# Attention followed by a squared-ReLU MLP: the second product moved into row tiles between the scores, two head pairs at a time

## The chip, the core and the metric

The kernel runs on one core of a Trainium2 chip. The metric is the device time of one execution in microseconds; the median of three runs is given. The profiled execution is a run of its own, so its span is a little shorter than the device time.

A core has a matrix engine (PE, with its weight loads PEld), a vector engine (DVE), an activation engine (ACT), GpSimd (POOL) and 16 DMA engines fed from queues. Matmuls write to PSUM, which has eight banks of 512 float32 columns on 128 partitions.

Two words are used throughout. A matmul in a *column tile* has at most 64 output partitions and uses half of the array's columns; two of them, to partitions 0 to 63 and 64 to 127, run side by side. A matmul in a *row tile* has a contraction of 64 and uses half of the array's rows; two of them, with their operands on partitions 0 to 63 and 64 to 127, run side by side. A *full* matmul uses the whole array. In the profile's groups the two numbers with a star are contraction and output partitions: `128*128` is full, `128*64` and `112*64` are column tiles, `64*112` is a row tile.

## The reference

Eight batches, twelve heads (six pairs), 448 tokens, head size 64; then an MLP of 768 to 2048 to 768 over all 3584 tokens.

```python
def _attn_ref(q, k, v):                       # (8, 12, 448, 64) each
    scale = 1.0 / np.sqrt(q.shape[-1])
    scores = scale * np.matmul(q, k.transpose(0, 1, 3, 2))
    m = np.max(scores, axis=-1, keepdims=True)
    e = np.exp(scores - m)
    attn = e / (np.sum(e, axis=-1, keepdims=True) + np.exp(-m) + 1e-09)
    return np.matmul(attn, v)

def _moe_ref(x, w_in, w_out):                 # (3584, 768), (768, 2048), (2048, 768)
    h = x @ w_in
    r = np.maximum(h, 0.0)
    return (r * r) @ w_out
```

The output is float32; the kernel works in float16 with float32 sums in PSUM. The denominator is the sum of exponentials plus one (in a scaled form), so no maximum is taken.

## The kernel before

One *unit* is one head pair of one batch (batch 0 is cut into two halves of its query tokens, so it gives twelve smaller units; batches 1 to 7 give 42 full units). A unit has four blocks of keys, `kk` 0 to 3, two of them in each call of `scores`.

```python
def exp(out_, in_):
    nc.scalar.activation(out=out_, in_=in_, func=AF.Exp, scale=scale)

def scores(u, et, c):                         # cut to the case of batches 2 to 7
    for kk in (2 * c, 2 * c + 1):
        sp = s_psum.tile([P, 2, 512], FP32, name="sp")       # two such tiles, two banks each
        for h in range(2):
            for odd in range(2):
                r = slice(64 * odd, 64 * odd + 64)
                ...
                nc.tensor.matmul(sp[:, odd, h * (S // 2):(h + 1) * (S // 2)],
                                 qk[r, which, kx:kx + 2 * P - 1:2], qk[r, 0, x:x + S // 2],
                                 start=True, stop=True)      # row tiles, 224 columns
        exp(...)                                             # one 112x896 activation

def values(u, et, xp, o=0):                                  # column tiles, 448 columns
    for kk in range(RUN):
        for h in range(2):
            nc.tensor.matmul(xp[64 * h:64 * h + 64, o:o + n], vns[b][:, 2 * pr + h, kk, :], ...)

def row_sums(us, sums):                                      # column tiles against ones
    zp = m_psum.tile([128, 512], FP32, name="mp")
    ...
    nc.scalar.activation(out=rcp[:, 0:m], in_=zp[:, 0:m], func=AF.Ln, bias=one_b)
    nc.scalar.activation(out=rcp[:, 0:m], in_=rcp[:, 0:m], func=AF.Exp, scale=-1.0)

def product(out_, lhsT, rhs, start, stop):
    if halved[0]:                                            # two column tiles
        for x in (0, 64):
            nc.tensor.matmul(out_[x:x + 64], lhsT[:, x:x + 64], rhs, start=start, stop=stop)
    else:                                                    # full
        nc.tensor.matmul(out_, lhsT, rhs, start=start, stop=stop)
```

The MLP is cut into generators: `mlp_in` is the first product (six matmuls for each tile of 128 hidden rows, then ReLU and square on DVE), `mlp_out` the second (sixteen matmuls for each tile of 128 tokens by 512 or 256 output columns, then one scaled copy on ACT and a store). `drain(ns)` takes so many nanoseconds of such matmuls between the parts of a unit:

```python
for i in range(2 * NPAIR, NU + 1):
    ...
    scores(u, et, 0)
    if i in transpose_at:
        transposes(*transpose_at[i])
    drain(share[0] * 0.45)                    # full matmuls
    scores(u, et, 1)
    ...
    rcp = row_sums(done, (ess.pop(i - 1),))
    values(prev, ets.pop(i - 1), xp)
    halved[0] = u is not None
    drain(share[0] * 0.15)                    # column tiles from here
    for step in range(3):
        add_chunks(u, et, es, half, step)     # sums of exponentials over kk, on DVE
        drain(share[0] * (0.15, 0.1, 0.15)[step])
    halved[0] = False
    normalise(done, xp, rcp)
    take_up(i - 1)
drain(1e12)                                   # what is left of the MLP after the last unit
```

PSUM: two `sp` tiles of two banks, one bank for `xp`, three for everything called `mp`. Queries and keys of batches 0 and 1 are transposed on PE; those of the other batches are staged in DRAM in float16 and read back by transposing DMAs.

Of the kernel before, what the change touches and what calls it, by code (L numbers as in the profile page):

```python
# [11 lines left out]
ALU = mybir.AluOpType  # L12
# [3 lines left out]
def kernel(  # L16
# [19 lines left out]
    ON_PE = (0, 1)  # L36
    COLS = H * S // 2 + 16

# [11 lines left out]
    e_pool = ctx.enter_context(tc.tile_pool(name="e", bufs=2))  # L50
    es_pool = ctx.enter_context(tc.tile_pool(name="es", bufs=3))
    z_pool = ctx.enter_context(tc.tile_pool(name="z", bufs=1))
    g_pool = ctx.enter_context(tc.tile_pool(name="g", bufs=2))
# [10 lines left out]
    wout = persist.tile([128, NFFB, DM], FP16, name="wout")  # L64

# [15 lines left out]
    def load_natural(b, p0, p1):  # L81

        raw = b == 0 and p1 <= 3
        for n, r in (("q", q_r), ("k", k_r)):
            src = r[b, :, 2 * p0:2 * p1]
            if raw:
                t = nat.tile([P, 2, RUN, D], FP32, name=f"{n}r{p0}")
                (nc.sync if n == "q" else nc.scalar).dma_start(out=t, in_=src)
            else:
                if p0 % 3 == 0:  # L90
                    whole[n] = nat.tile([P, NPAIR, RUN, D], FP16, name=f"{n}n{p0 // 3}")
                t = whole[n][:, 2 * (p0 % 3):2 * (p0 % 3 + p1 - p0)]
                nc.gpsimd.dma_start(out=t, in_=src)
            for pr in range(p0, p1):
                naturals[n, b, pr] = t[:, 2 * (pr - p0):2 * (pr - p0) + 2]
# [5 lines left out]
    def load_wout(i, n):  # L101
        w = NFFB // n
        nc.gpsimd.dma_start(out=wout[:, i * w:(i + 1) * w, :], in_=wout_r[:, i * w:(i + 1) * w, :])
# [40 lines left out]
    def transposes(b, pr):  # L144
        tp = m_psum.tile([128, 2, 512], FP16, name="mp")
# [82 lines left out]
    def row_sums(us, sums):  # L228
# [3 lines left out]
        zp = m_psum.tile([128, 512], FP32, name="mp")  # L232
        for j, (u, es) in enumerate(zip(us, sums)):
            total = es[:, 0:2 * n]
            if n < S:
                total = total.rearrange("p (h n) -> p h n", h=2)
            for h in range(2):
                nc.tensor.matmul(zp[64 * h:64 * h + 64, j * n:(j + 1) * n], ones, of_head(total, u, h),  # L238
                                 start=True, stop=True)
# [5 lines left out]
    def normalise(us, xp, rcp):  # L245
        b, pr, q0, n = us[0]
        if b // 2 not in xts:
            xts[b // 2] = xt_pool.tile([128, DCH, 2 * S], FP16, name="xt")
        c = b % 2 * S + q0
        if len(us) == 1:  # L250
            nc.vector.tensor_mul(xts[b // 2][:, pr, c:c + n], xp[:, 0:n], rcp[:, 0:n])  # L251
        else:
            two = [t[:, 0:2 * n].rearrange("p (j n) -> p j n", j=2) for t in (xp, rcp)]
            nc.vector.tensor_mul(xts[b // 2][:, pr:pr + 2, c:c + n], *two)  # L254


    gts = {}
    halved = [False]

    def product(out_, lhsT, rhs, start, stop):  # L260

        if halved[0]:
# [5 lines left out]
    def mlp_in(t0, n):  # L268
        gt = gts[t0] = []
        xt, x0 = xts[t0 // (2 * S)], t0 % (2 * S)  # L270
        per = max(1, 512 // n) if n < 384 else 1
        for f0 in range(0, NFFB, per):
            hp = m_psum.tile([128, 512], FP32, name="mp")
            for j in range(per):
                fb = f0 + j
                for dc in range(DCH):
                    product(hp[:, j * n:(j + 1) * n], win[:, dc, fb * 128:(fb + 1) * 128],
                            xt[:, dc, x0:x0 + n], start=(dc == 0), stop=(dc == DCH - 1))
                    if j < per - 1 or dc < DCH - 1:
                        yield n / 2.4  # L280
            m = per * n
            rt = r_pool.tile([128, 512], FP16, name="rt")
            if t0 == 0 and f0 == 8:
                nc.scalar.activation(out=rt[:, 0:m], in_=hp[:, 0:m], func=AF.Relu)
            else:
                nc.vector.tensor_scalar(out=rt[:, 0:m], in0=hp[:, 0:m], scalar1=0.0, scalar2=None, op0=ALU.max)  # L286
            g = g_pool.tile([128, 512], FP16, name=f"g{f0}")
            nc.vector.tensor_mul(g[:, 0:m], rt[:, 0:m], rt[:, 0:m])  # L288
            for j in range(per):
                gt.append(g[:, j * n:(j + 1) * n])  # L290
            yield n / 2.4

    def store(c, ot, n0, n1):
        end = c + 128
        while c < end:
# [3 lines left out]
            t, p = c % S // (S // step), c % (S // step)  # L299
# [5 lines left out]
    def mlp_out(t0, n):  # L305
        gt = gts.pop(t0)
        for ts in range(n // 128):
            ot = osb_pool.tile([128, DM], FP32, name="ot")
            for n0, n1 in ((0, 512), (512, DM)):
                op = m_psum.tile([128, 512], FP32, name="mp")  # L310
                for fb in range(NFFB):
                    product(op[:, 0:n1 - n0], gt[fb][:, ts * 128:(ts + 1) * 128], wout[:, fb, n0:n1],
                            start=(fb == 0), stop=(fb == NFFB - 1))
                    if fb < NFFB - 1:
                        yield (n1 - n0) / 2.4
                nc.scalar.activation(out=ot[:, n0:n1], in_=op[:, 0:n1 - n0], func=AF.Copy, scale=OUT_SCALE)  # L316
                if n1 == DM or t0 + ts * 128 + 128 == NT:
                    store(t0 + ts * 128, ot, 0 if n1 < DM or t0 + ts * 128 + 128 < NT else n0, n1)
                if n1 < DM:
                    yield (n1 - n0) / 2.4  # L320
            yield (DM - 512) / 2.4
# [23 lines left out]
    load_v(1, 0, 3)  # L345
    for i in range(4):
        load_wout(i, 4)
    load_v(1, 3, 6)


    work, left = [], [0.0]

    def queue(part, t0, n):
        work.append((mlp_in if part == 1 else mlp_out)(t0, n))
        left[0] += (NFFB * DCH * n if part == 1 else n // 128 * NFFB * DM) / 2.4

    def drain(ns):
        while work and ns > 0:
            got = next(work[0], None)
            if got is None:  # L360
                work.pop(0)
            else:
                ns -= got
                left[0] -= got
# [6 lines left out]
    ready = {NPAIR - 1: [(1, 0, 128)],  # L371
             2 * NPAIR - 1: [(1, 128, 256), (2, 0, 128), (2, 128, 256)]}
    t0 = 384
    for b in range(1, B):
        n = 384 if b % 2 == 0 else 512
        ready[(b + 2) * NPAIR - 1] = [(1, t0, n), (2, t0, n)]
        t0 += n

    transpose_at = {pr - 1: (0, pr) for pr in range(1, NPAIR)}
    for pr in range(NPAIR):  # L380
        transpose_at[NPAIR + 2 + pr] = (1, pr)
# [6 lines left out]
    def take_up(i):  # L388
        if i in ready:
            for part in ready[i]:  # L390
                queue(*part)
            share[0] = left[0] / NPAIR

    share = [0.0]
    ets, ess = {}, {}
    xp = None
# [8 lines left out]
    for i in range(2 * NPAIR):  # L405
        u = units[i]
        et = ets[i] = e_pool.tile([P, RUN * 2 * S], FP16, name="et")
        es = ess[i] = es_pool.tile([P, 2 * S], FP16, name="es")
        half = e_pool.tile([P, 1024], FP16, name="half")
# [3 lines left out]
        halved[0] = True  # L413
# [3 lines left out]
        if i == NPAIR:  # L417
            values(units[i - 1], ets.pop(i - 1), xp, units[i - 1][3])
            rcp = row_sums(two, (ess.pop(i - 2), ess.pop(i - 1)))
            normalise(two, xp, rcp)  # L420
            take_up(i - 1)
            share[0] = left[0] / (NPAIR + 1)
# [9 lines left out]
        if two and i != NPAIR:  # L432
            rcp = row_sums(two, (ess.pop(i - 2), ess.pop(i - 1)))
        if i and i != NPAIR:
            values(units[i - 1], ets.pop(i - 1), xp, (i - 1) % 2 * units[i - 1][3])
        drain(share[0] * 0.3)
# [4 lines left out]
        drain(share[0] * 0.25)  # L441
        halved[0] = False


    for i in range(2 * NPAIR, NU + 1):
        u = units[i] if i < NU else None
# [4 lines left out]
        if u:  # L451
            b, pr = u[0:2]
            if pr == 0 and b + 1 < B:
                load_v(b + 1, 0, NPAIR)
                stage(b + 1)
            et = ets[i] = e_pool.tile([P, RUN * 2 * S], FP16, name="et")
            es = ess[i] = es_pool.tile([P, 2 * S], FP16, name="es")
            half = e_pool.tile([P, 1024], FP16, name="half")
            scores(u, et, 0)
            if i in transpose_at:  # L460
                transposes(*transpose_at[i])
            drain(share[0] * 0.45)
            scores(u, et, 1)
        if first:
            done = units[i - 2:i]
            values(prev, ets.pop(i - 1), xp, prev[3])
            rcp = row_sums(done, (ess.pop(i - 2), ess.pop(i - 1)))
# [4 lines left out]
        halved[0] = u is not None  # L472
        drain(share[0] * 0.15)
        for step in range(3):
            if u:
                add_chunks(u, et, es, half, step)
            drain(share[0] * (0.15, 0.1, 0.15)[step])
        halved[0] = False
        normalise(done, xp, rcp)
        take_up(i - 1)  # L480
        if u and pr == 2 and b + 1 < B:
            transposed_loads(b + 1)
    drain(1e12)
# [28 lines left out]
```

## Time and profile before

| | |
|---|---|
| device time, median of 3 | 431.62 us (431.44 to 432.69) |
| span of the profiled execution | 428.3 us |
| busy: PE, PEld, DVE, ACT, POOL | 417.4, 247.1, 242.6, 244.9, 33.2 us |
| matmuls | 4099 |
| DMA | 47.57 MB, mean 111 GB/s |

How to read it: two matmuls that run side by side overlap in time, and even a single stream overlaps its matmuls' ends with the next ones' starts, so the mean duration of a matmul is not what it costs. What a matmul costs is the distance from its start to the next start. Idle time is listed with what ended it (`<-` the releaser). The line numbers (L190 scores, L225 values, L238 row sums, L264 products in column tiles, L266 full products, L158 exponentials, L241 and L242 the logarithm and exponential of the denominators) are those of the kernel before.

### The profile page before, as it was taken

Reading aid. Unit: us, or ns where it says so; the run is one execution under the profiler, and the core shown is the slowest. Engines: PE = TensorE matmul, PEld = TensorE weight load, DVE = VectorE, ACT = ScalarE, POOL = GpSimd, SP = SyncE. Lnnn points to the kernel's source line nnn. Section 1 sums busy time; section 2 is a strip of 40 time slices with the busy share of each in tenths; the row PEclk is TensorE's granted clock in tenths of the full one; section 3 lists DMA queues with packets and bytes.
Section 4 is the critical chain, followed back from the end, with each engine's and each line's share of the span. In section 5 each row is a group of like instructions: output and inputs, shape, how many; then the busy total and the mean of one; then the engine's idle time right before and its main releaser. Section 6 shows DMA issues by size and latency. Waiting matters only on the chain.

```text
span 428.3 us, 9350 instructions
## 1 busy us (share of the span) xinstructions
PE 417.4 (97%) x4099; PEld 247.1 (58%) x4099; DVE 242.6 (57%) x466; ACT 244.9 (57%) x346; POOL 33.2 (8%) x52
## 2 busy tenths in 40 slices
PE   7888999999999999999999999999999999999996
PEld 3566665644566666554566665655556566564464
DVE  4757793378722786258832497348762379328700
ACT  3878777754456656674466755765555664740011
POOL 6541100000000100010000100030000000000000
PEclk9989999999999999999999999999999999999999
DMA  9999999599221993279712696049902200010022
GB/s 187 197 197 202 211 221 170 126 194 187 46 66 47 182 189 57 75 125 193 109 38 75 110 197 120 38 74 203 177 13 75 75 2 2 37 64 12 0 73 75
DMA packets 79129, 47.57 MB, mean 111 GB/s; under 512 B 50672, under 2 KB 75120, under 8 KB 78704
## 3 DMA queue, kind: packets, MB, share of 16 engines
q0 software_dynamic: 24160, 22.17, 32.5%
q1 hardware_dynamic: 54208, 24.11, 26.3%
q10 hardware_dynamic: 720, 0.69, 0.6%
q8 instruction: 32, 0.52, 0.5%
q14 instruction: 9, 0.07, 0.1%
HBM read 45.71 MB, written 19.32 MB: 152 GB/s over the span
## 4 chain that ended last, share of the span: by engine, by line
PE 89%; DMA 8%; ACT 1%; DVE 1%; issue 0%; POOL 0%; POOLq 0%
PE mp L266 37%; PE mp L264 31%; PE sp L190 9%; PE xp L225 7%; DMA kn<-in_k_dram 3%; PE mp L238 3%; DMA win<-in_moe_w_in_dram 3%; DMA vn<-in_v_dram 2%; PE sp L178 1%; ACT et L158 0%; POOL win L99 0%; DVE half L207 0%; DVE xt L254 0%; ACT rcp L242 0%; DVE rt L286 0%
## 5 line engine op out<-in xcount | busy, mean ns | idle before, releaser
L158 ACT ACTIVATE et<-sp 112x896 f16<-112x896 f32 (+2 forms) x192 | 166.1, 914 | 111.6 <-PE sp L190 92.1
L286 DVE TENSOR_SCALAR rt<-mp 128x512 f16<-128x512 f32 (+1 forms) x123 | 78.0, 634 | 34.8 <-PE mp L264 23.8
L266 PE MATMUL mp<-xt,win 128*128 128x512 f16 (+3 forms) x423 | 82.2, 347 | 0.5 <-DVE xt L254 0.5
L266 PE MATMUL mp<-wout,g 128*128 128x512 f16 (+1 forms) x471 | 82.3, 330 | 0.0
L264 PE MATMUL mp<-xt,win 128*64 128x512 f16 (+3 forms) x882 | 74.7, 321 | 1.1 <-DVE xt L254 1.1
L264 PE MATMUL mp<-wout,g 128*64 128x256 f16 (+1 forms) x850 | 71.9, 322 | 0.0
L266 PEld LDWEIGHTS <-g 128*128 128x128 f16 x471 | 44.4, 98 | 33.9 <-issue 2.2
L316 ACT ACTIVATE ot<-mp 128x512 f32<-128x512 f32 (+1 forms) x56 | 27.3, 487 | 63.4 <-PE mp L266 51.7
L264 PEld LDWEIGHTS <-win 128*64 128x64 f16 x882 | 48.3, 112 | 23.7 <-issue 2.1
L266 PEld LDWEIGHTS <-win 128*128 128x128 f16 x423 | 39.3, 98 | 37.2 <-issue 2.6
L264 PEld LDWEIGHTS <-g 128*64 128x64 f16 x850 | 47.7, 110 | 19.4
L203 DVE TENSOR_TENSOR half<-et 112x896 f16<-112x896 f16 x42 | 26.1, 622 | 54.5 <-ACT et L158 54.4
L203 DVE TENSOR_TENSOR es<-et 112x896 f16<-112x896 f16 x42 | 26.1, 622 | 49.1 <-ACT et L158 49.1
L288 DVE TENSOR_TENSOR g<-rt 128x512 f16<-128x512 f16 (+1 forms) x124 | 49.5, 399 | 4.2
L225 PE MATMUL xp<-et,vn 112*64 112x448 f16 (+2 forms) x432 | 46.1, 335 | 1.1 <-DVE xt L254 1.0
L190 PE MATMUL sp<-qk 64*112 64x224 f16 x576 | 42.8, 268 | 0.0
L190 PEld LDWEIGHTS <-qk 64*112 64x112 f16 x576 | 26.9, 128 | 25.4 <-issue 25.4
L241 ACT ACTIVATE rcp<-mp,one_b 128x448 f32<-128x448 f32 (+2 forms) x48 | 30.6, 638 | 1.7 <-PE mp L238 1.7
L225 PEld LDWEIGHTS <-vn 112*64 112x64 f16 x432 | 24.1, 110 | 12.3 <-issue 2.5
L242 ACT ACTIVATE rcp<-rcp 128x448 f32<-128x448 f32 (+2 forms) x48 | 27.7, 577 | 1.5
L79 POOL DMA_DIRECT2D vn<-in_v_dram x10 | 9.0, 901 | 241.3 <-PE xp L225 229.4
L251 DVE TENSOR_TENSOR xt<-xp,rcp 128x448 f16<-128x448 f32 x42 | 25.9, 617 | 2.4 <-ACT rcp L242 2.4
(40 smaller groups left out, 152.2 us busy)
## 6 DMA issues: line engine op xcount, KB each, us to landing
out_dram<-ot SPq DMA_DIRECT2D x11, 384.0 KB, 2.3
vn<-in_v_dram POOLq DMA_DIRECT2D x6, 672.0 KB, 9.0
stage_q<-in_q_dram POOLq DMA_DIRECT2D x5, 676.0 KB, 11.6
stage_k<-in_k_dram POOLq DMA_DIRECT2D x5, 676.0 KB, 14.4
win<-in_moe_w_in_dram POOLq DMA_DIRECT2D x8, 384.0 KB, 13.7
wout<-in_moe_w_out_dram POOLq DMA_DIRECT2D x4, 768.0 KB, 19.6
out_dram<-ot SPq DMA_DIRECT2D x8, 288.0 KB, 2.6
out_dram<-ot SPq DMA_DIRECT2D x8, 192.0 KB, 2.7
```

Of the source, the lines that this page charges most:

```text
L158: nc.scalar.activation(out=out_, in_=in_, func=AF.Exp, scale=scale)
L190: nc.tensor.matmul(sp[:, odd, h * (S // 2):(h + 1) * (S // 2)], qk[r, which, kx:kx + 2 * P - 1:2], qk[r, 0, x:x + S // 2], start=True, sto ...
L203: nc.vector.tensor_add((es, half[:, 0:2 * S])[step], e[:, 2 * step], e[:, 2 * step + 1])
L225: nc.tensor.matmul(xp[64 * h:64 * h + 64, o:o + n], vns[b][:, 2 * pr + h, kk, :], of_head(chunk(et, u, kk // 2, kk), u, h), start=(kk == 0 ...
L241: nc.scalar.activation(out=rcp[:, 0:m], in_=zp[:, 0:m], func=AF.Ln, bias=one_b)
L242: nc.scalar.activation(out=rcp[:, 0:m], in_=rcp[:, 0:m], func=AF.Exp, scale=-1.0)
L251: nc.vector.tensor_mul(xts[b // 2][:, pr, c:c + n], xp[:, 0:n], rcp[:, 0:n])
L264: nc.tensor.matmul(out_[x:x + 64], lhsT[:, x:x + 64], rhs, start=start, stop=stop)
L266: nc.tensor.matmul(out_, lhsT, rhs, start=start, stop=stop)
L286: nc.vector.tensor_scalar(out=rt[:, 0:m], in0=hp[:, 0:m], scalar1=0.0, scalar2=None, op0=ALU.max)
L288: nc.vector.tensor_mul(g[:, 0:m], rt[:, 0:m], rt[:, 0:m])
L316: nc.scalar.activation(out=ot[:, n0:n1], in_=op[:, 0:n1 - n0], func=AF.Copy, scale=OUT_SCALE)
```

## The change

The second product of the MLP now runs a whole batch behind the first, so its input, `gs`, is kept in a ring of two batches. From batch 2 on two units are taken at a time, a *cell*. A cell has a first part in which all matmuls are in row tiles (the four calls of `scores`, and between them the second product, whose contraction of 128 is cut into two of 64 that go to two PSUM banks and are added afterwards on DVE), and a second part in which all are in column tiles (values of the cell before, first product, row sums).

Its purpose is that the array keeps one way of tiling for long stretches: before, every call of `scores` stood alone between column-tiled or full matmuls.

```diff
-    ON_PE = (0, 1)
+    ON_PE = (0, 1, 2)
+    HALF = DM // 2
...
-    e_pool = ... bufs=2 ; es_pool = ... bufs=3 ; z_pool = ... bufs=1
+    e_pool = ... bufs=4 ; es_pool = ... bufs=2 ; z_pool = ... bufs=2
+    RING = 2 * S
+    gs = persist.tile([128, NFFB, RING], FP16, name="gs")
...
+    def mp_tile(dtype=FP32):                 # from the first cell on every 4th tile is xp's bank
+        if joined[0] >= 0:
+            joined[0] += 1
+        pool, name = (x_psum, "xp") if joined[0] > 0 and joined[0] % 4 == 0 else (m_psum, "mp")
...
+    def tile_out(tok, n0):                   # 128 tokens x 384 output columns
+        rows = mode[0] == ROWS2
+        op = mp_tile()
+        lo = mp_tile() if rows else None
+        for fb in range(NFFB):
+            g = gs[:, fb, tok % RING:tok % RING + 128]
+            if rows:
+                for x, o in ((0, op), (64, lo)):
+                    nc.tensor.matmul(o[:, 0:w], g[x:x + 64], wout[x:x + 64, fb, n0:n0 + w],
+                                     start=(fb == 0), stop=(fb == NFFB - 1))
+            else:
+                product(op[:, 0:w], g, wout[:, fb, n0:n0 + w], ...)
+        if rows and n0 == 0:
+            nc.vector.tensor_scalar(out=ot[...], in0=op[...], scalar1=OUT_SCALE, ...)
+        else:
+            nc.scalar.activation(out=ot[...], in_=op[...], func=AF.Copy, scale=OUT_SCALE)
+        if rows:
+            nc.vector.scalar_tensor_tensor(out=ot[...], in0=lo[...], scalar=OUT_SCALE, in1=ot[...], ...)
...
-    for i in range(2 * NPAIR, NU + 1):       # as above
+    for i in range(2 * NPAIR, 3 * NPAIR):    # batch 1: as before, but only the first product is drained,
+        ...                                  # and the row sums take two parts (two matmul pairs)
+    for c in range((NU - 3 * NPAIR) // 2):   # batches 2 to 7: cells
+        scores(ua, ea, 0)
+        rows(11)                             # 11 of a tile's 16 steps of the second product, row tiles
+        scores(ua, ea, 1)
+        add_chunks(ua, ea, sa, ha, 0)
+        rows(11)
+        scores(ub, eb, 0)
+        add_chunks(ua, ...1) ; add_chunks(ua, ...2)
+        rows(10)
+        scores(ub, eb, 1)
+        add_chunks(ub, eb, sb, hb, 0)
+        mode[0] = COLS2
+        for at in pending:                   # the two units of the cell before
+            ...
+            xp = mp_tile()
+            values(units[at], ets.pop(at), xp)
+            normalise([units[at]], xp, rcps.pop(at))
+        if b in ON_PE and pr + 2 < NPAIR:    # batch 2
+            transposes(b, pr + 2) ; transposes(b, pr + 3)
+        if pr == 0:
+            run(ins, len(ins))
+            queue((b - 1) * S, S)            # the first product of the batch before: 16 tiles of 448 columns
+            if b > 2:
+                run(outs)                    # one more tile of the second product, in column tiles
+            ... transposed_loads(b + 1); hold(b + 1); load_v(b + 1); stage(b + 2)
+        n = (3, 7, 6)[pr // 2]
+        run(ins, n - 3)
+        add_chunks(ub, ...1) ; add_chunks(ub, ...2)
+        run(ins, 2)
+        for at in (i, i + 1):
+            rcps[at] = row_sums([units[at]], (ess.pop(at)[0:1],))
+        run(ins, 1)
+        pending = [i, i + 1]
+    ...                                      # last values, then full products until all is done
```

Smaller parts: batch 2 is transposed on PE too (from natural loads, as batch 1); the second half of batch 1's transposes comes one unit later; nothing of the MLP is drained in unit 6; the output weights are loaded in two column halves and later; the first raw loads of queries and keys share buffers with the exponentials.

## Prediction

> **What bounds the kernel now.** I read the busy table, then the chain of waits, then the groups by form, then the timeline of a steady stretch start by start, and last the table by stretches.
>
> ```profile
> PE 417.4 (97%) x4099; PEld 247.1 (58%) x4099; DVE 242.6 (57%) x466; ACT 244.9 (57%) x346; POOL 33.2 (8%) x52
> ...
> PE 89%; DMA 8%; ACT 1%; DVE 1%; issue 0%; POOL 0%; POOLq 0%
> ```
>
> PE is the bound from about 50 us to the end; the chain has 8% of DMA, all of it in the first 40 us. The other engines have 43% in hand, on average. So only fewer or cheaper PE starts can help, and only new waits of PE can harm. What a start costs is seen in the timeline (start, length, engine, line, operation, tiles, count):
>
> ```profile
> 151.10 0.59 PE L190 MATMUL sp<-qk 64*112 64x224 f16 x8
> 151.71 0.38 PE L238 MATMUL mp<-es,ones 112*64 112x448 f16 x2
> 151.90 0.95 PE L225 MATMUL xp<-et,vn 112*64 112x448 f16 x8
> 152.66 3.28 PE L264 MATMUL mp<-xt,win 128*64 128x384 f16 x38
> 155.87 0.59 PE L190 MATMUL sp<-qk 64*112 64x224 f16 x8
> 156.40 0.34 PE L266 MATMUL mp<-xt,win 128*128 128x384 f16 x1
> ```
>
> The values' four column pairs take 0.76 us from start to start (151.90 to 152.66), 189 ns a pair of 448 columns. That is 448/2.4 plus 2.5 ns, and so it is for all forms: full matmuls of 512 columns start every 216 ns, column pairs of 256 every 109. At this rate a call of scores, four row pairs of 224 columns, should take 0.38 us; from 155.87 to 156.40 it takes 0.53. Taking single records, start to start, in the whole trace: a column or full matmul of 512 columns before a row tile takes 309 ns where it takes 213 to 216 before its own kind (96 more); the first row pair of a call takes 140 where the next take 94 (46 more, its weights are not loaded ahead); the last takes 186 to 188 (94 more). One call of scores therefore costs 0.236 us beyond its columns.
>
> The ledger of the 428.3 us, from the instruction order with N/2.4 + 2.5 ns for each full matmul and for each pair: columns 382.6; 106 row blocks (212 changes into or out of row tiles) at 0.236, 25.0; what is left, some 21, is nearly all in the first 50 us (waits for loads and for ACT) and the last 3.3 us (the last copy and store). From 50 to 425 us the waits of PE that this does not explain come to 3 us.
>
> **What the Trainium skill says.** "TensorEngine Tiling (Array Packing)", section Key Properties: changing the tiling mode, not just the tile, drains the engine. The trace agrees, and gives the 94 to 96 ns that the page lacks. The same page, Gotcha 1: PSUM Pressure: different row tiles must write to different banks; hence `op` and `lo` and the second pass over PSUM. No run of before shows that. "TensorE: Matmul & The Clock Gate", section Back-to-back issue gap, gives N/2.4 + 2.5 ns for an isolated warm matmul, as the trace has it, and also 131 ns for N=512 in a real stream; the trace has 216, so the measurement decides. Its section on the array's architecture calls ACT and DVE strict FIFO; the ACT records here stand in program order too. That matters below.
>
> **The change part by part.**
>
> *Changes of tiling.* In the order of the changed program I count 102 changes into or out of row tiles, 51 blocks for 106. 55 x 0.236 = 13.0 us less, all on PE's path.
>
> *Columns.* Batch 2's transposes: 96 more matmuls of 112 columns, in pairs (112/2.4 + 2.5)/2 = 24.6 ns each, 2.4 us. Row sums of five units in two parts: ten more matmuls of 448 columns at 94.6 ns, 0.9 us. The second product in row pairs of 384 columns costs 162.5 ns a step, as it would full. Together +3.2 us (385.8 for 382.6).
>
> *Head.* At 37.5 us unit 11 waits for the keys of batch 1's second half:
>
> ```profile
> 39.00 0.39 PE L149 MATMUL mp<-ident,kn 112*64 112x112 f16 x8 [1.35 <-DMA kn<-in_k_dram]
> ```
>
> These transposes now come a unit later. -1.3 us.
>
> *Batch 1.* It had 25.6 us of MLP to fill its six units (the first product of 256 tokens 10.2, the second of 384 tokens 15.4); now 12.8 (320 tokens), of which some 2.5 are left over. A unit is then 4.8 us of PE (two calls of scores with their changes 1.2, transposes 0.4, first product 2.0, row sums and values 1.1) against ACT's 4.4: four exponentials at 0.81 and the denominator's pair at 0.67 + 0.48. The 0.81 comes from the timeline, where a pair of exponentials takes 1.72 us and one alone 0.91; 0.67 and 0.48 are starts to next starts of L241 and L242. So ACT is nearly as long as PE, and the second call's second tile waits 0.2 to 0.5 us for the second exponential. +2 us.
>
> *Cells.* PE needs, for a whole batch of three cells, 47 us, ACT some 28 and DVE 37, so the average is harmless. The order inside is not. At the end of a cell stand two row sums, one tile of the first product, and then the next cell's first scores, 11 row steps, second scores. ACT is given, in this order, Ln, Exp, Ln, Exp of the denominators and then the exponentials.
>
> ```profile
> L158 ACT ACTIVATE et<-sp 112x896 f16<-112x896 f32 x168 | 144.6, 914 | 101.4 <-PE sp L190 92.1 <-PE sp L178 9.2
> L241 ACT ACTIVATE rcp<-mp,one_b 128x448 f32<-128x448 f32 x42 | 26.8, 639 | 1.6 <-PE mp L238 1.6
> L242 ACT ACTIVATE rcp<-rcp 128x448 f32<-128x448 f32 x42 | 24.2, 577 | 1.3
> ```
>
> From the first row sum's start, PE reaches the last four matmuls of the second scores after 0.38 (row sums) + 1.14 (six pairs of 448) + 0.14 (change) + 0.38 (scores) + 1.79 (11 x 0.1625) + 0.19 = 4.02 us. They need the second `sp` tile, free when the second exponential has ended: 0.44 (a row sum's 375 ns and the semaphore, 60 ns as between scores and exponentials in the head) + 2 x (0.67 + 0.48) + 0.81 + 0.91 + 0.06 = 4.53 us. PE waits 0.5 us once a cell; afterwards ACT has 2.2 us for each 1.6 and catches up. In the cells with 7 and 6 tiles DVE makes part of the same wait earlier: the two sums of exponentials (1.07 us) stand before a ReLU (0.65) whose bank the last tile needs, about 0.3 us late; what PE waits there it no longer waits at ACT. The first cell has no denominators before it, so 17 cells; I take 0.4 us for 0.5, as each chain is a sum of six terms and only lateness of PE elsewhere can shorten it: 17 x 0.4 = 6.8, rounded to +7.
>
> *First cell.* It must wait for the last unit's denominator and product of batch 1 before the first product can use it: +1 us.
>
> *Extra eviction.* 36 tiles of the second product are in row tiles, each with one more DVE pass of 128x384, and half of them with the first copy on DVE too. DVE's 128x384 pass from PSUM takes 552 to 557 ns (rows L286 and L254), so 54 x 0.555 = 30 us more on DVE, 273 or so of 430. Off the path, as the four banks that go round are each free about 1 us before their turn.
>
> Sum: 431.6 - 13.0 + 3.2 - 1.3 + 2 + 7 + 1 = 430.5; I say 430.
>
> **The rivals.**
>
> *ACT's queue takes nothing (gain kept).* If PE reaches the second scores later than I count, or exponentials start sooner, the 7 us vanish: 423 to 424. For it: ACT is idle 43% of the time. Against: FIFO order and the durations are measured.
>
> *ACT and DVE waits spread.* If every call of scores waits, not only the second, or DVE's later sums hold up the row sums (their slack in the cell of 7 tiles is only 0.1 us by my count), another 0.3 us in each of 18 cells and more in batch 1: 436 to 438. For it: two `sp` tiles are all there are, and the four calls now follow each other within 7 us, in which ACT needs 6.5. Against: 11 row steps and a call are 2.2 us for 1.6 of exponentials.
>
> *Row tiles of 128 columns stream slower.* Weight loads of 64x128 might not hide behind 160 ns. The loads of 64x112 (128 ns) hide behind 94 ns now. If a step cost 20 ns more, 576 x 20 ns = 11.5 us: 441. Unlikely.
>
> *The output weights come late.* They are now queued behind batch 2's natural loads. In the table by stretches the DMA engines move 198 GB/s in the first 50 us; at that rate 1.57 MB (a half, in half precision) take 8 us and the two natural loads ahead of each 3.5. Counted on from 39 us and 50 us, when the loads before have landed or their buffers come free, I get about 54 and 66 us for the halves, needed at about 71 and 75 us. A few us if I am wrong.
>
> **Range and chances.** The gain of the changes is firm (10 us net of the columns), the head and batch 1 are worth 1 us either way, and the cells decide: from none of the wait to twice of it is 423 to 438. Range 421.5 to 437. Faster by over 2% means under 423.0: the first rival with a little luck, 0.18. Slower by over 2% means over 440.2: two of the others together, 0.07.
>
> **What would show it.** Row blocks of some 7 us with starts every 162 ns, and about 0.24 us per block instead of per call: right on the gain. PE idle with ACT `et` as releaser, 0.3 to 0.5 us, at the second scores of each cell and 5 to 8 us in all: right on the wait. None there, and a time near 423: the chain through ACT is wrong. PE idle with DVE as releaser over 5 us, or row steps above 170 ns, or a DMA wait for `wout` at 70 to 80 us: a rival won. DVE's busy time should be near 275 us and ACT's near 235.

## The result, and the profile after

The changed kernel takes 427.59 us (median of 4, 427.55 to 427.89) for 431.53 (431.27 to 432.69): a ratio of 0.9905, with a 95% interval of 0.9887 to 0.9924. The span of the profiled execution is 426.0 us for 428.3.

The busy table and the chain of waits of the changed kernel:

```profile
PE 410.8 (96%) x4715; PEld 271.7 (64%) x4715; DVE 278.1 (65%) x537; ACT 236.5 (56%) x328; POOL 36.5 (9%) x58
...
PE 75%; DVE 10%; ACT 6%; DMA 5%; issue 2%; POOL 1%; ACTq 0%; POOLq 0%
```

PE is still the bound, but the chain now passes through DVE and ACT for 16% of the span, where it had 2%. DVE is busy 36 us longer; the 36 second passes over PSUM are 20 us of that (558 ns each). PE's busy time fell by 6.6 us though it has 616 matmuls more.

The timeline of PE in the first part of a cell (L194 is scores, L329 the second product in row tiles, L229 values; the lines of the second product in the middle, which alternate between two tile names and so stand one by one, are left out):

```profile
119.24 0.59 PE L194 MATMUL sp<-qk 64*112 64x224 f16 x8
119.67 1.95 PE L329 MATMUL mp<-wout,gs 64*128 64x384 f16 x22
121.46 0.59 PE L194 MATMUL sp<-qk 64*112 64x224 f16 x8
121.84 1.02 PE L329 MATMUL mp<-wout,gs 64*128 64x384 f16 x10
...
123.63 0.59 PE L194 MATMUL sp<-qk 64*112 64x224 f16 x8
...
125.64 0.61 PE L194 MATMUL sp<-qk 64*112 64x224 f16 x8
126.18 1.71 PE L229 MATMUL mp<-et,vn 112*64 112x448 f16 x16
```

Read it start to start. The second call takes 0.38 us (121.46 to 121.84), just its columns; the kernel before needed 0.53 and another 0.1 ahead of it. The first call takes 0.43: the 46 ns of its first weights. The 22 matmuls of eleven row steps take 1.79 us (119.67 to 121.46), 163 ns a step. Only the last call pays for a change, 0.54 us (0.04 of it is a wait: in the version without the cells' waits, shown below, it takes 0.50). Scores of 112 output partitions and products of 128 stand side by side without a drain.

What the gain is given back to, in the table of waits (who, for whom: us in total, times, longest):

```profile
PE mp L279 <- DVE xt L258: 1.9, 2, 1.0
PE mp L279 <- DVE rt L299: 1.5, 10, 0.2
PE sp L194 <- ACT et L162: 1.2, 5, 0.3
...
PE mp L153 <- DMA kn<-in_k_dram: 1.0, 1, 1.0
...
PE xp L279 <- DVE rt L299: 0.5, 3, 0.2
```

These idle times run from the modelled end of a matmul, which lies some 0.2 us behind the point where the next could start; start to start each wait costs more. The first line and the DMA's lie in the first 45 us, where the first product of batch 0 waits for the attention output of its last pairs (at 22 and at 44 us) and a transpose for its keys. Of the other two kinds, one each from the timelines: first the end of a cell of seven tiles (L279 first product, L243 row sums), then the second call of scores in the second cell of a batch, behind the cell of three tiles:

```profile
149.53 0.55 PE L279 MATMUL mp<-xt,win 128*64 128x448 f16 x4
149.90 0.62 PE L243 MATMUL mp<-es,ones 112*64 112x448 f16 x4
150.68 0.38 PE L279 MATMUL xp<-xt,win 128*64 128x448 f16 x2 [0.15 <-DVE rt L299]
```

```profile
136.42 0.36 PE L194 MATMUL sp<-qk 64*112 64x224 f16 x4
137.03 0.40 PE L194 MATMUL sp<-qk 64*112 64x224 f16 x4 [0.25 <-ACT et L162]
```

The row sums should take 0.38 us and take 0.78: the tile behind them waits for a bank whose ReLU is late. With single records, it is 0.34 to 0.35 us in the cells of seven and six tiles, twelve in all. The second half of the scores should follow after 0.19 us and follows after 0.61: 0.41 to 0.42 us, in the second cell of batches 3 to 7, five in all (the row sums that cause it stand at the end of the first cell). Together 12 x 0.35 + 5 x 0.41 = 6.2 us.

### The profile page after: what moved, and what is told of

The parts are those of the page before. It is cut to its first block, busy times and chain, and to the rows that moved or that the text cites. A ratio compares the mean times of both kernels' runs of the same rounds, so it can differ in the third digit from the quotient of the medians.

```text
span 426.0 us, 10689 instructions
## 1 busy us (share of the span) xinstructions
PE 410.8 (96%) x4715; PEld 271.7 (64%) x4715; DVE 278.1 (65%) x537; ACT 236.5 (56%) x328; POOL 36.5 (9%) x58
## 4 chain that ended last, share of the span: by engine, by line
PE 75%; DVE 10%; ACT 6%; DMA 5%; issue 2%; POOL 1%; ACTq 0%; POOLq 0%
PE mp L279 18%; PE mp L329 15%; PE mp L281 11%; PE xp L279 6%; PE sp L194 5%; PE mp L229 5%; PE xp L329 5%; DVE rt L299 4%; DMA kn<-in_k_dram 4%; ACT et L162 3%; PE xp L281 3%; PE xp L229 3%; PE sp L182 3%; DVE es L209 2%; DMA vn<-in_v_dram 2%; DVE half L207 2%
## 5 line engine op out<-in xcount | busy, mean ns | idle before, releaser
L279 PE MATMUL mp<-xt,win 128*64 128x448 f16 (+2 forms) x1260 | 113.2, 324 | 4.1 <-DVE xt L258 1.9
L279 PEld LDWEIGHTS <-win 128*64 128x64 f16 x1536 | 84.8, 110 | 50.4 <-issue 9.1
L329 PE MATMUL mp<-wout,gs 64*128 64x384 f16 x864 | 103.1, 322 | 0.0
L329 PEld LDWEIGHTS <-gs 64*128 64x128 f16 x1152 | 70.8, 94 | 18.5
L299 DVE TENSOR_SCALAR rt<-mp 128x448 f16<-128x448 f32 (+2 forms) x104 | 62.8, 604 | 23.2 <-PE mp L279 19.7
L301 DVE TENSOR_TENSOR gs<-rt 128x448 f16<-128x448 f16 (+2 forms) x132 | 50.8, 385 | 4.9 <-ACT rt L297 0.4
L329 PE MATMUL xp<-wout,gs 64*128 64x384 f16 x288 | 52.6, 322 | 0.0
L194 PE MATMUL sp<-qk 64*112 64x224 f16 x480 | 36.7, 261 | 1.2 <-ACT et L162 1.2
L194 PEld LDWEIGHTS <-qk 64*112 64x112 f16 x480 | 29.5, 128 | 9.2 <-issue 7.3
L229 PEld LDWEIGHTS <-vn 112*64 112x64 f16 x432 | 22.7, 109 | 15.2 <-issue 4.6
L281 PE MATMUL mp<-wout,gs 128*128 128x384 f16 x192 | 31.9, 326 | 0.0
L279 PE MATMUL xp<-xt,win 128*64 128x448 f16 x276 | 30.0, 353 | 0.5 <-DVE rt L299 0.5
L182 PE MATMUL sp<-qk 64*112 64x448 f16 (+2 forms) x192 | 24.0, 321 | 1.2 <-ACT et L162 0.5
## 6 DMA issues: line engine op xcount, KB each, us to landing
stage_q<-in_q_dram POOLq DMA_DIRECT2D x4, 676.0 KB, 11.2
```

Source lines behind the costliest of these rows:

```text
L182: nc.tensor.matmul(sp[:, h, o:o + n], qk[r, 1, x + P * kk:x + P * kk + P], qk[r, 0, x + q0:x + q0 + n], start=True, stop=True)
L301: nc.vector.tensor_mul(gs[:, f0:f0 + per, t0 % RING:t0 % RING + n], r, r)
L329: nc.tensor.matmul(o[:, 0:w], g[x:x + 64], wout[x:x + 64, fb, n0:n0 + w], start=(fb == 0), stop=(fb == NFFB - 1))
```

## The experiments

Ten kernels that tell the reasons apart. Times are medians; ratios are to the kernel before, run on the same chip. The theory: changes of tiling cost 0.24 us a row block and pay as counted; what is lost is lost to the order of work in a cell, at DVE and ACT. The rivals: the gain is the small rearrangement of the head; the second pass on DVE, or DVE's load as a whole, costs what the tiling gains; the waits are latencies that no order removes.

**The second product as full matmuls between the scores.**

```diff
     def rows(n):
-        mode[0] = ROWS2
+        mode[0] = FULL
```

> The changed kernel, with the 32 steps of the second product between the scores taken as full matmuls (one bank, no second pass on DVE) instead of row tiles. Columns are the same: a row pair and a full matmul of 384 columns both cost 162.5 ns. Theory (changes of tiling pay): each of the 18 cells has four row blocks for one, 54 x 0.236 us = 12.7 us more, less about 1 us of waits that the later scores hide: 439, between 437.5 and 440.5. Rival (the gain comes from the head of the kernel, the tiling is neutral): 427 to 430. Rival (the additional pass on DVE costs about what the tiling gains): 427 to 433.

439.17 us, ratio 1.0177 (1.0152 to 1.0202). PE's timeline:

```profile
121.93 0.59 PE L194 MATMUL sp<-qk 64*112 64x224 f16 x8
122.45 1.96 PE L281 MATMUL xp<-wout,gs 128*128 128x384 f16 x11
124.34 0.59 PE L194 MATMUL sp<-qk 64*112 64x224 f16 x8
124.87 0.99 PE L281 MATMUL xp<-wout,gs 128*128 128x384 f16 x5
```

Each call is back to 0.52 or 0.53 us, and eleven steps take 1.89 us for 1.79. Over the four calls and three groups of steps a cell is 0.68 us longer, 0.227 us for each of its three added blocks; 18 x 0.68 = 12.2 us, of which 5 x 0.2 = 1.0 are hidden, as ACT's wait falls from 0.41 to 0.21 us. That is 11.2 of the 11.9 us by which the span grows (437.9 for 426.0); the other 0.7 lie in the head, where unit 12 starts so much later in this trace. The row tiles of the second product are worth 11 to 12 us. The head's code was the same, and there was no second pass on DVE (with the full matmuls ACT makes all the first copies, too); both rivals fall.

**The head alone, in the kernel before.**

```diff
-        transpose_at[NPAIR + 2 + pr] = (1, pr)
+        transpose_at[NPAIR + 2 + pr + pr // 3] = (1, pr)
...
-            share[0] = left[0] / (NPAIR + 1)
+            share[0] = left[0] / NPAIR
...
-        drain(share[0] * 0.3)
+        if i > NPAIR:
+            drain(share[0] * 0.3)
...
-        drain(share[0] * 0.25)
+        if i > NPAIR:
+            drain(share[0] * 0.25)
```

> The kernel before, with only the small parts of the change in its first 40 us: the second half of batch 1's transposes one unit later, nothing of the MLP drained in unit 6. By the two traces unit 12 starts at 38.2 us instead of 41.1, so the theory that the head's part is 2.9 us gives 428.6. The prediction's own term, 1.3 us, gives 430.2. Rival (the head is the whole gain): 427.6 or less.

429.52 us, ratio 0.9955 (0.9936 to 0.9974): 2.1 us, between the two expectations. It is more than half of the net gain, so the rival was not far off in size; but the run above shows that the tiling's part is larger and is then spent on other things. The traces show less: the span is 427.6 us for 428.3. Unit 12 starts at 38.66 us, 2.5 us earlier, but in unit 13 PE then waits 1.55 us instead of 0.51 for the attention output of batch 0's last pairs, and 1.5 of the 2.5 us are a stretch of lower clock that, of these two, only the trace of the kernel before has (it is shown in the next section). So what the edit itself is worth stays open; between 0.6 and 2.1 us were measured.

**More row steps ahead of the second scores.**

```diff
-        rows(11)
+        rows(13)
         scores(ua, ea, 1)
         add_chunks(ua, ea, sa, ha, 0)
-        rows(11)
+        rows(10)
         scores(ub, eb, 0)
...
-        rows(10)
+        rows(9)
         scores(ub, eb, 1)
```

> The changed kernel, with 13, 10 and 9 row steps between the four calls of scores instead of 11, 11 and 10: the second call comes 0.32 us later after the denominators. Theory (ACT's queue, Ln and Exp ahead of the exponentials, makes PE wait 0.41 us at the second scores in the first cell of a batch, and nothing in the others, where PE already waited for DVE): 5 x 0.32 = 1.6 us less, 426.0. Rival (the wait is a slow PE start or scattered): no change, 427.6. Should the fewer steps before the third and fourth call uncover waits of ACT there, it gets slower than 427.6.

428.66 us, ratio 0.9926 (0.9897 to 0.9956): 1.1 us slower than the changed kernel. The second call behind the cells of three tiles takes 0.47 us where it took 0.80, so the wait for ACT is shortened as expected; but the fourth call now waits, in every cell:

```profile
158.64 0.73 PE L194 MATMUL sp<-qk 64*112 64x224 f16 x8
159.30 0.38 PE L229 MATMUL mp<-et,vn 112*64 112x448 f16 x2
```

0.66 to 0.70 us for 0.49 to 0.54: some 18 x 0.13 = 2.3 us lost for 5 x 0.33 = 1.6 won. The wait for ACT is moved about in the first part of the cell by shifting steps there, not removed.

**The two late sums of exponentials apart.**

```diff
-        run(ins, n - 3)
+        first = min(1, n - 3)
+        run(ins, first)
         add_chunks(ub, eb, sb, hb, 1)
+        run(ins, n - 3 - first)
         add_chunks(ub, eb, sb, hb, 2)
         run(ins, 2)
```

> The changed kernel, with the first of the two late sums of exponentials on DVE moved ahead by up to three tiles of the first product, so that they no longer stand together before a ReLU that PE needs. If the 0.35 us that PE waits for DVE in two cells of three were all that holds it, 12 x 0.35 = 4.2 us less: 423.4. Theory (two waits in a row: without DVE's wait PE arrives 0.35 us earlier at the second scores and waits there for ACT, about 0.4 us, in all cells): 427 to 427.6, PE waits for ACT 17 times. Rival (DVE as a whole is too full, the order doesn't matter): 427.6 with the wait for DVE still there.

427.28 us, ratio 0.9900 (0.9876 to 0.9924). The wait for the ReLU is gone, and nothing is gained. Its table of waits:

```profile
PE sp L194 <- ACT et L162: 3.8, 15, 0.3
```

The expectation of the run before names the first cell for ACT's wait; its cause lies there, but PE waits in the cell after. It was five times, now it is fifteen, every cell of batches 3 to 7, and one more in batch 2: the second call takes 0.80 us in each. Two waits in a row on one path: the 0.35 us at DVE had hidden the 0.41 at ACT.

**Both sums early, and two tiles behind the row sums.**

```diff
-        run(ins, n - 3)
+        early = min(2, n - 3)
+        run(ins, early // 2)
         add_chunks(ub, eb, sb, hb, 1)
+        run(ins, early - early // 2)
         add_chunks(ub, eb, sb, hb, 2)
-        run(ins, 2)
+        run(ins, n - 2 - early)
         for at in (i, i + 1):
             rcps[at] = row_sums([units[at]], (ess.pop(at)[0:1],))
-        run(ins, 1)
+        run(ins, 2)
```

> The changed kernel, with both late sums of exponentials moved ahead among the first tiles of the first product, and the row sums one tile earlier, so that two tiles (2.27 us) stand after them instead of one (1.14). Theory (the cells' waits are the order alone: DVE's 0.35 us in two cells of three, ACT's 0.41 us in the third): the 1.14 us cover the 0.41, and nothing of the product waits for the sums; 12 x 0.35 + 5 x 0.41 = 6.2 us less, 421.4, with PE waiting for neither in the cells. Rival (row sums now come before the sums of exponentials are done, and PE waits there instead): 425 to 428.

421.61 us, ratio 0.9780 (0.9734 to 0.9827): 6.0 us less than the changed kernel with the same instructions. From the start of the second cell to the end its trace is 7.1 us shorter (333.9 for 341.0): the 6.2 us, and most of the rest is the fourth call, which takes 0.50 us for 0.54 in each cell of batches 3 to 7. The first cell is 0.8 us longer. PE's timeline at the end of a cell and the start of the next:

```profile
148.19 0.55 PE L243 MATMUL mp<-es,ones 112*64 112x448 f16 x4
148.57 1.30 PE L279 MATMUL mp<-xt,win 128*64 128x448 f16 x12
149.70 1.30 PE L279 MATMUL xp<-xt,win 128*64 128x448 f16 x12
150.93 0.59 PE L194 MATMUL sp<-qk 64*112 64x224 f16 x8
151.36 1.95 PE L329 MATMUL mp<-wout,gs 64*128 64x384 f16 x22
153.15 0.55 PE L194 MATMUL sp<-qk 64*112 64x224 f16 x8
153.53 0.65 PE L329 MATMUL mp<-wout,gs 64*128 64x384 f16 x6
```

Row sums 0.38, second call 0.38 (153.15 to 153.53). The rival's wait is there once, in the first cell, where the sums are late and the cell has only three tiles:

```profile
83.14 0.38 PE L243 MATMUL xp<-es,ones 112*64 112x448 f16 x2 [1.50 <-DVE es L209]
```

**Without the second pass.** Left out: the half of the contraction that the second bank holds.

```diff
-        if rows:
-            nc.vector.scalar_tensor_tensor(out=ot[:, n0:n0 + w], in0=lo[:, 0:w], scalar=OUT_SCALE,
-                                           in1=ot[:, n0:n0 + w], op0=ALU.mult, op1=ALU.add)
```

> The changed kernel without the additional pass of DVE over the second product's other bank: the output lacks that half of the contraction in the row-tiled tiles. Theory (20 us of DVE that lie beside PE's work): 427.6, within 0.5. Rival (DVE's load is what makes its later work late): the 0.35 us waits vanish or shrink, 423.5 to 426.

427.80 us, ratio 0.9913 (0.9889 to 0.9938). DVE is busy 263.0 us for 278.1, and the tile behind the row sums waits as long as it did (0.34 us). The pass costs nothing; it is the order of DVE's work that makes PE wait, and not this part of its load.

**The transposes of batch 1 yet later.**

```diff
-        transpose_at[NPAIR + 2 + pr + pr // 3] = (1, pr)
+        transpose_at[NPAIR + 3 + pr] = (1, pr)
...
-        if i == NPAIR + 4:
+        if i == NPAIR + 5:
             load_natural(2, 0, 3)
```

> The changed kernel, with all transposes of batch 1 one unit later (units 9 to 14 without the gap), and the first natural loads of batch 2 one unit later with them. In the trace unit 8 waits 1.2 us for the keys that it transposes. Theory (a wait for a load that is simply not needed so early): 1.2 us less, 426.4. Rival (the head is set by ACT and the loads behind, the wait turns up elsewhere): 427.6.

426.98 us, ratio 0.9898 (0.9854 to 0.9942): 0.6 us less, half of the wait. The other half turns up where the second load of keys is used, as PE's timeline shows:

```profile
38.53 0.39 PE L153 MATMUL mp<-ident,kn 112*64 112x112 f16 x8 [0.88 <-DMA kn<-in_k_dram]
```

Here the rival is partly right: the loads set the pace of the head.

**Together.** The edit of the two sums (the one with two tiles behind the row sums), the edit just shown, and in the first cell the left-over tiles ahead of the transposes.

```diff
+        if pr == 0:
+            run(ins, len(ins))
         if b in ON_PE and pr + 2 < NPAIR:
             transposes(b, pr + 2)
```

> The last-but-two and the last edit together, and in the first cell the left-over tiles of the first product ahead of batch 2's transposes instead of behind (there PE waits 0.6 us for a bank that the logarithm of the last unit of batch 1 holds behind two exponentials). Theory: 6.2 + 1.2 + 0.5 = 7.9 us less than the changed kernel, 419.7. Rival (the head's part is nothing): 420.9.

420.58 us, ratio 0.9764 (0.9703 to 0.9826), 0.9 us short of the sum: the head gave 0.6 for 1.2, and the edit of the first cell nothing, as PE then waits for the last unit's product (0.7 us) instead of for the bank.

**The first cell in another order.** On top of the last one:

```diff
         rows(11)
+        if c == 0:
+            rcps[i - 1] = row_sums([units[i - 1]], (ess.pop(i - 1),))
         scores(ua, ea, 1)
...
-        run(ins, n - 2 - early)
+        late = 1 if c == 0 else 2
+        run(ins, n - late - early)
...
-        run(ins, 2)
+        run(ins, late)
```

> The version with the edits of the sums, the head and the first cell together (420.58 us), with two things changed in the first cell alone: the row sums of batch 1's last unit go between the cell's first and second scores instead of behind all four, and the cell's own row sums keep one tile behind them instead of two. In that version's trace PE waits 1.7 us for a sum of exponentials at the first cell's row sums and 0.7 us for the last unit's product. Theory (both waits are only the order of that cell): 1.2 + 0.7 less, one more row block, 0.24, against it: 418.9. Rival (DVE is full there and PE waits at the next step): 420 to 420.6.

419.14 us, ratio 0.9725 (0.9692 to 0.9759). 1.4 us of the expected 1.7; the row block there costs more than counted, as the third call of scores then waits 0.6 us. This is the best version, 2.7% faster than the kernel before and 2.0% (419.14/427.59) than the changed one.

**The denominators without their exponential.** On the version with the sums apart; the output is then multiplied by the logarithm instead of the reciprocal.

```diff
-        nc.scalar.activation(out=rcp[:, 0:m], in_=rcp[:, 0:m], func=AF.Exp, scale=-1.0)
```

> The version with the sums spread (427.28 us, PE waits for ACT at the second scores of all cells but the first), without the exponential that makes a reciprocal of the denominator's logarithm: the output is scaled wrongly, all else is the same. Theory (the four activations of the denominators ahead of the exponentials are the wait): ACT's chain is 2 x 0.48 us shorter, more than the 0.42 us that PE waits, so 17 x 0.42 = 7.1 us less, 420.1. Rival (the wait is the latency of scores, exponentials and their banks, whatever stands before): 427.3, or as far as batch 1 gains, 426.

420.42 us, ratio 0.9742 (0.9700 to 0.9785), 6.9 us less than with it. From the start of the second cell to the end its trace is 7.3 us shorter (333.3 for 340.6), and PE no longer waits for ACT at the second scores. The wait is ACT's queue: what stands ahead of the exponentials, and not the latency between scores and exponentials.

## Why the prediction was right, and where it missed

The mechanism held for the tiling and for the cells. In batch 1 and in the head the sizes came near, but for other reasons than predicted. The stated 430 us are 2.4 us too high, the sum of 430.5 is 2.9 too high. In terms of the span, which the ledger was made in, it gave 428.3 - 13.0 + 3.2 - 1.3 + 2 + 7 + 1 = 427.2 us; measured are 426.0. In the table, a stretch of a trace less its columns and 0.236 us for each row block is counted as waits.

| step | predicted | measured |
|---|---|---|
| changes of tiling | -13.0 | 54 blocks put back cost 11.6 in time, 12.2 in the cells with what they hide: 0.227 a block for 0.236 |
| columns | +3.2 | +3.2 by the matmuls in the traces; not tested apart; 163 ns a row step as assumed |
| head, waits to the start of unit 12 | -1.3 | -2.1 in the traces, of which 1.5 the clock and 0.5 the first loads; -2.1 in time, alone |
| batch 1 | +2 | 38.2 to 69.7 us, 31.5 for 28.5 of columns and changes; in the kernel before 38.9 for 37.0: +1.1 |
| waits in the cells | +7 | 6.2 counted one by one, 7.1 against the trace without them |
| first cell | +1 | 2.0 in the trace (0.63, 0.43, 0.53 and 0.37 us at four starts) |

With 13.0 for the changes, 6.2 for the cells and 0.3 more at the end of the program, the measured terms give -2.3 us, the difference of the spans. That the first cell was put 1.0 us too low and batch 1 0.9 too high cancels in the sum; this is luck.

*The tiling* was right in mechanism and size. The drain that "TensorEngine Tiling (Array Packing)", section Key Properties, states is there at each change and, as that section says, not between tiles of one mode.

*The head* came out larger for a reason that the prediction didn't have. Unit 12 starts 2.9 us earlier (38.2 for 41.1); 0.6 of that are columns and 0.2 a row block that now come later, and 0.5 passed before the first scores, which start at 6.5 us instead of 7.0 (in the traces with this head they start at 6.5 to 7.3). Another 1.5 us are PE's clock. The table by stretches of the kernel before has a granted clock (the column behind POOL) of 0.50 here, and the same work, values and then first product, is slower in its timeline than in that of the changed kernel, which comes second:

```profile
24.60:27.90 3.30, 3.30 (x44) 2.52 (x44) 1.25 (x3) 2.05 (x2) 1.49 (x3) 0.50 1.46 197
```

```profile
25.97 1.07 PE L225 MATMUL xp<-et,vn 112*64 112x256 f16 x8
26.82 1.17 PE L264 MATMUL mp<-xt,win 128*64 128x128 f16 x18
```

```profile
28.34 0.60 PE L229 MATMUL xp<-et,vn 112*64 112x256 f16 x8
28.78 0.67 PE L279 MATMUL mp<-xt,win 128*64 128x128 f16 x18
```

Start to start, the values take 0.85 us for 0.44, and the products behind them 1.10 for 0.60. The trace of the changed kernel has no such stretch between 5 us and its last matmul. These terms make up the 2.9 us; what the head waits for loads and other engines is in sum as long as before. The wait for the second half of the keys (1.5 us, predicted as 1.3) is gone, and a new one of 1.2 us for the first half came up.

*Batch 1* waits in other places than predicted. The second call's wait for the second exponential, 0.2 to 0.5 us in each unit by the prediction, is 0.06 us in three units, 0.2 in one and 0.44 in one. The longest wait is 1.2 us in unit 13, where the first product needs the attention output of batch 0's last pairs (0.7 in the kernel before).

*The cells* were right as a sum and nearly as a division: "What PE waits there it no longer waits at ACT" is what the spread sums showed. I had 0.5 us once a cell and took 0.4; it is 0.35 at DVE in twelve and 0.41 at ACT in five. So the sign that I had named, ACT as the releaser in every cell, was there in five, and in sixteen once the two sums stood apart. "ACT's queue takes nothing" was the rival nearest to the measured time, and it is wrong: had the waits been absent, the time would have been 421.6, as it is when they are removed. "ACT and DVE waits spread" is wrong too: with 11, 11 and 10 steps the third call doesn't wait and the fourth 0.04 us; with 13, 10 and 9 the fourth waits. For the other two, row steps take 163 ns, and no transfer of the output weights is waited for.

*The rest*, 1.7 us between the sum and the measured time, is no part of the change. I put the differences on the median of the time (431.6), but took the ledger from a profiled execution that was 1.4 us faster (430.17 us); the other 0.3 is the changed kernel's profiled execution against its median. The kernel before scatters from 429.8 to 434.0 us over all runs, the changed one here within 0.4. The clock has a part in it. Of 26 executions of the kernel before beside the experiments, 24 have a mean granted clock of 0.992 to 0.996, and of 49 with the new head, five. The five of the kernel before at 0.992 took 432.6 to 434.0 us, the 19 at 0.995 and 0.996 took 429.8 to 432.1, and the two at 0.999 and 1.0 took 430.1 and 430.4. So the new head seems to avoid the stretch, and this may be most of the 2.1 us of the head alone; but why, and what else scatters the kernel before, is open. It is open, too, how much of the 3.9 us the change would gain at one clock: by the two traces, less the clock and the first loads, it is some 0.3 us, and against the two executions at 0.999 and 1.0 it is 2.5 and 2.8.

## What to carry to other kernels

Where tiled matmuls of two kinds alternate, count the changes and put one kind together, with other work that can be done in that same tiling between its parts; splitting a contraction in two for that cost no PE time here, and the second pass over PSUM that lay beside it cost none either. Then write down, for each call that needs a buffer back, the chain of the other engine from the last point where it is known to be idle, in its queue's order, with start-to-start times: here sums of five or six terms foretold waits of 0.4 us to within 0.1. Waits that follow each other on one path hide each other, so an edit that removes one and gains nothing has not shown that it was harmless. And look at the granted clock before a shorter stretch is put down to an edit.

## What the runs showed of the hardware

Row pairs in two streams slip against each other. In the cell shown above the two matmuls of a pair start 1 to 3 ns apart up to the second call of scores, and 51 or 52 ns apart from that call's last pair on (121.75 and 121.80 us), through the products and the third call; a step still takes 163 ns.

A weight load's length is not that of its columns: 128 columns took 94 ns in row tiles and 98 ns full, 112 columns 128 ns, and 64 columns in column tiles 110 ns. "TensorE: Matmul & The Clock Gate", section Weight-path perf modes, describes a fast load for exactly 128 columns; these lengths agree with that, and with column tiles not having it. None set the pace here: row steps of 384 columns go at 163 ns with 94 ns loads, scores of 224 at 94 ns with 128 ns loads.
